# List scatters tied to matmul groups, spectral tiles with pairs of rows innermost, and a new step order

## The chip, the cores and the metric

The kernel runs on one core of a Trainium2 chip. The metric is the time of one execution on the device in microseconds (us); lower is better. The core has five engines that run side by side and meet only through semaphores: TensorE (PE; its weight loads are listed apart as PEld), VectorE (DVE), ScalarE (ACT), GpSimd (POOL) and SyncE (SP). SP, ACT and POOL also issue the transfers between the chip's memory and SBUF, the memory on the core. Matmul results go to PSUM, of which the program uses eight banks of 128 partitions by 512 floats.

## The reference

The kernel computes two things in a row, all in 32-bit floats. First a spectral layer over `x` (8 sequences of 1856 rows of 256 floats):

```python
X = np.fft.rfft(x, axis=1)
Yr = Xr @ w_r - Xi @ w_i + b_r
Yi = Xr @ w_i + Xi @ w_r + b_i
# both soft-thresholded: sign(Y) * max(|Y| - 0.01, 0)
y = np.fft.irfft(Y, n=x.shape[1], axis=1)
```

Then a mixture of experts over the 14848 rows of `y`: each row picks the best of 4 groups and in it the best of 4 experts by two small products and softmaxes; its expert computes `relu(row @ w1) @ w2` (256 to 1024 to 256), and the result is scaled with the two softmax weights.

## The kernel before

**Spectral part.** The sequences are taken in four pairs (`pr`). A sequence of 1856 is 58 by 32, so the transforms become two steps of small matmuls with a transpose between them. Forward: `lead_mm` (letter c in the order, `a_mm` there) multiplies with the 58-point table into two PSUM banks; `turn_a` (d) transposes each bank on VectorE in blocks of 32 into the tile `zys[pr]`, whose free axes are frequency row k (32), sequence of the pair (2) and channel (128). Then for each of 15 pairs of rows k: `f_mm` (e) with the table T; `f_high`, `f_neg`, `f_low`, `f_lneg` (f, g, h, i) split the result into a rounded high part and a rest; `m_bias` (j) and `m_mm` (k), 24 matmuls with the weights' high and low parts; two thresholds `m_relu` (m, n) on ScalarE and their difference `m_sub` (o) on VectorE, written back into `zys`. Backward: `b_mm` (r), its transposes `b_turn` (s) into the tile `vs`, whose axes are row r, sequence, channel; and `p_mm` (v). `p_out` (w) stores the rows to memory (`ys_d`), `p_turn` (x) transposes them, `p_copy` (y on ScalarE, z on VectorE) copies them out.

**Routing.** `g_mm` (G) computes the choice's scores for half a pair, `g_turn` (H) transposes them, and `route_g` (R, one small operation per letter) picks group and expert and counts, for each row, its place in its expert's list. `scatter` (S) then writes one column of 128 rows (row number and weight) into the lists in memory (`lst`) with an indirect DMA on POOL; there are 16 for half a pair and 128 in all. At most three are on their way: each waits for the third one before it to land.

**Early jobs and the rest.** Before all pairs are routed, eight jobs of 256 rows for experts 0 to 3 start from the first entries of the lists: `list_load` (I, on SP), `list_convert` (Z), `e_fetch` (F, two indirect DMAs on POOL), `e_turn` (T), `e_high`, `e_low` (X, Y), `up_mm` (U), `up_high`, `up_low` (A, B), `down_mm` (D), `down_act`, `down_add` (E, J) and `down_out` (K, an indirect DMA on POOL). `w_high` and `w_low` (W, V) split the experts' weights; `load_steps` (l) loads inputs and weights on SP. `last_lists` (L) loads the final lists, `first_rows` (M) fetches the first rows of the job that follows. After the order's end a list of jobs over all 16 experts runs, written in program order (lines 1088 to 1140).

**What sets the order.** The string `ORDER` is a list of 1694 letters; each runs the next step of its kind. A step's instructions are put on TensorE, ScalarE, VectorE and SP in just this order. POOL is not among the engines ordered by hand (`engines`, line 542): its instructions follow the program too, but a scatter starts when its inputs are there and the third scatter before it has landed. So a letter S says when a scatter is written down, not how far TensorE is when it starts. At the start, before the order, the first pair's transposes and the tables are made: T is zeroed and filled by POOL from `traw` in three slices of rows (line 357), `wl`, the low part of the weights, is computed on POOL at line 371.

Of the kernel before, what the change touches and what calls it, by code (L numbers as in the profile page):

```python
# [42 lines left out]
jhdicmnReldfokghjdiRRcnRmRedfovghjkwdwRiRSRvSmnSxweowSzxjxzSxfzkyShgiSSvmSnewokwSjSfSghcmSixnldSeydjcSofxgShkydidcmneldf
ocghjkdiddcnmeldfovghjkwdwivnmewoxwxzjxzkfghivmnewokwjfghGmniojxzfezgxHxyhkyRiRRRRRRvRmRnRewRokwRRjRRfRRgRhvmRRieRwRRwRr
nxfskogyhjsiRxmRxzneRyxojkyRRfRgRhrmRSRiensSfsroSgjGsSshSrHiSesRrsSRRkSRsRSsRRSRRrmRSnRkRSsRfRogSjRhSRriRsmSRneRsfSkRRgo
jRhRisrRmnesfoRkghjsiRemRnvRRfokwRghwRijRSRxmxzSenzfvSoghjkSwwSiSxmxSzenzSfvogShjkwwSiSSxmxzenSzfvoSghjkwSwSixmxzenzfvoI
ghjGwwixHxyZkRyRRRRRRRRvmRnRkRwowRfRRRgxRhmvyRiRxwRRkwzRnRRoRvmnRRwwoxxRFyxRyxRyRyrRFRGssWSWVrWHSWVTSWRsWTRsSWrVWSsXRsSr
RYSsRsrSRRsSRsrSRVSRlUsSRsrARSVRURsSRsSrARRBWSsUWRBWRsUWRRAVvRXBARVwRwxxyBRyRVvRlYDwRwVRvVRxVwDwzRVvWRWlRSVUWVSWVUEVSAJl
# [73 lines left out]
def spectral_moe(ctx: ExitStack, tc: tile.TileContext, x, wri, bri, wgate, w1, w2, cst, out):  # L122
    nc = tc.nc
# [114 lines left out]
    pend, sent = [], []  # L238
# [79 lines left out]
    def new_z():  # L318
        return big.tile([128, KP, 2, 128], F32, name="big")
# [16 lines left out]
    def turn_a(pr, i, bt, o):  # L336
        return nc.vector.transpose(out=zys[pr][:, :, bt, i * 16:i * 16 + 16].rearrange("p k d -> p d k"),
                                   in_=o.rearrange("p (r d) -> p d r", d=16))
# [858 lines left out]
```

## Time and profile before

| what | value |
|---|---|
| median of 3 runs | 1264.16 us (1260.18 to 1267.79) |
| profiled execution, its own time | 1264.4 us |
| its span, first to last instruction | 1262.6 us |
| TensorE busy | 1180.3 us, 93% |
| VectorE busy | 706.8 us, 56% |
| ScalarE busy | 599.5 us, 47% |
| POOL busy | 398.1 us, 32% |
| TensorE clock granted, mean | 0.963 |

The page gives each engine's busy time, then the same in 40 slices of 31.6 us, among them the clock that TensorE was granted. Matmuls overlap, so TensorE's busy share says little on how much work it does; the number of instructions in a stretch says more. A timeline row gives an instruction's start, its length, its engine and line, and in brackets the engine's idle time before it with what ended it: another engine's instruction, a DMA, "remote" (something that is no instruction of the program) or "issue" (nothing that the profile shows). L462 and higher up to L531 are the listed experts, L808 to L831 the early jobs, L244 the scatters.

### The profile page before, as it was taken

The numbers are of one execution on the slowest core, as the hardware profiler recorded it, in microseconds if no ns is written. First come the engines' busy times: TensorE is split into PE (matmuls) and PEld (weight loads), VectorE is DVE, ScalarE is ACT, GpSimd is POOL, SyncE is SP. The second block draws the span as 40 slices with busy tenths as digits, with TensorE's granted clock in tenths as the row PEclk, the third lists the DMA queues.
The fourth block names the chain that finished last, engine by engine and source line by source line (L and its number), as shares of the span: only waits on it lengthen the run. The fifth ranks groups of instructions, "written<-read, shape, count | busy, mean of one in ns | idle before, by whom it ended". The sixth has DMA issues, their size and how long they took to land. (4 is left out here: it accounts for less than half of the span.)

```text
span 1262.6 us, 20533 instructions
## 1 busy us (share of the span) xinstructions
PE 1180.3 (93%) x7620; PEld 963.0 (76%) x7620; DVE 706.8 (56%) x1525; ACT 599.5 (47%) x1435; POOL 398.1 (32%) x447
## 2 busy tenths in 40 slices
PE   8999999989989496689999999999999999999996
PEld 4897786758677173478888888887887988888886
DVE  5657767735855485343557465455455473474452
ACT  2675574547556144132346455444454463463442
POOL 3000005230441515664442434333333323433421
PEclk8999999979989698899999999999999999999998
DMA  9300420122012053303133243452452445335300
GB/s 382 113 1 1 151 118 2 68 84 101 18 52 86 16 204 103 96 18 104 55 117 133 82 165 110 161 190 88 160 194 94 146 143 202 121 126 219 118 26 27
DMA packets 42361, 138.70 MB, mean 110 GB/s; under 512 B 17446, under 2 KB 19756, under 8 KB 31890
## 3 DMA queue, kind: packets, MB, share of 16 engines
q1 hardware_dynamic: 21458, 88.95, 19.7%
q0 software_dynamic: 15904, 31.48, 7.5%
q10 hardware_dynamic: 4896, 16.92, 3.4%
q8 instruction: 61, 1.00, 0.3%
q14 instruction: 42, 0.34, 0.1%
HBM read 103.24 MB, written 35.00 MB: 109 GB/s over the span
## 5 line engine op out<-in xcount | busy, mean ns | idle before, releaser
L523 PE MATMUL py<-big,hh 128*128 128x512 f32 x824 | 298.7, 403 | 0.0
L462 PE MATMUL ph<-xth,big 128*128 128x384 f32 (+1 forms) x896 | 256.9, 362 | 2.6 <-DVE hl L468 1.6
L244 POOL DMA_INDIRECT lst<-ent,sloti x128 | 128.2, 1001 | 353.7 <-DVE mx_g L160 176.1
L524 PE MATMUL py<-big,hl 128*128 128x256 f32 x824 | 231.6, 281 | 0.0
L468 DVE SCALAR_TENSOR_TENSOR hl<-ph,hh 128x256 fp32r<-128x256 f32 x448 | 151.3, 380 | 79.6 <-ACT hh L466 69.0
L523 PEld LDWEIGHTS py<-big,hh 128*128 128x128 f32 x824 | 155.0, 188 | 37.7 <-issue 3.2
L462 PEld LDWEIGHTS ph<-xth,big 128*128 128x128 f32 x896 | 165.1, 188 | 23.4 <-PE ph L462 2.7
L466 ACT ACTIVATE hh<-ph 128x256 fp32r<-128x256 f32 x448 | 137.9, 373 | 84.9 <-PE ph L462 80.8
L462 PE MATMUL ph<-xtl,big 128*128 128x384 f32 (+1 forms) x448 | 161.5, 361 | 0.3 <-DVE xtl L450 0.3
L509 POOL DMA_INDIRECT out_dram<-yo,si_f x96 | 97.6, 1017 | 184.4 <-DVE yo L531 158.9
L524 PEld LDWEIGHTS py<-big,hl 128*128 128x128 f32 x824 | 154.9, 188 | 0.1
L429 POOL DMA_INDIRECT xg<-ys_d,gi_f x96 | 93.6, 975 | 181.6 <-PE pg L445 158.0
L530 ACT ACTIVATE yo<-py,ent_f 128x256 f32<-128x256 f32 x96 | 45.6, 475 | 194.0 <-PE py L524 153.8
L531 DVE SCALAR_TENSOR_TENSOR yo<-py,ent_f,yo 128x256 f32<-128x256 f32 x96 | 46.4, 483 | 162.6 <-ACT yo L530 113.8
L642 PE MATMUL pw<-wh,xh 128*128 128x256 f32 x480 | 126.5, 300 | 2.3 <-issue 2.1
L642 PE MATMUL pw<-wl,xh 128*128 128x256 f32 x480 | 120.3, 287 | 1.8 <-issue 1.7
L642 PEld LDWEIGHTS pw<-wh,xh 128*128 128x128 f32 x480 | 93.8, 195 | 22.9 <-issue 12.7
L412 DVE TENSOR_TENSOR big<-xt,big 128x512 fp32r<-128x512 f32 x160 | 109.1, 682 | 0.0
L411 ACT CAST big<-xt 128x512 fp32r<-128x512 f32 x160 | 104.3, 652 | 0.0
L642 PEld LDWEIGHTS pw<-wl,xh 128*128 128x128 f32 x480 | 93.9, 196 | 2.3 <-issue 2.3
L462 PEld LDWEIGHTS ph<-xtl,big 128*128 128x128 f32 x448 | 84.2, 188 | 8.2 <-DVE xtl L450 0.6
L671 DVE STREAM_TRANSPOSE big<-bank 128x512 f32<-128x512 f32 x64 | 65.8, 1067 | 33.7 <-remote 21.7
(196 smaller groups left out, 1872.2 us busy)
## 6 DMA issues: line engine op xcount, KB each, us to landing
xt<-in_w_dram SPq DMA_DIRECT2D x48, 1024.0 KB
ys_d<-ysb ACTq DMA_DIRECT2D x32, 512.0 KB
big<-in_w_dram SPq DMA_DIRECT2D x16, 1024.0 KB
big<-in_x_dram SPq DMA_DIRECT2D x8, 1024.0 KB
xt<-in_x_dram SPq DMA_DIRECT2D x8, 1024.0 KB
lst<-ent,sloti POOLq DMA_INDIRECT x128
lst<-zero SPq DMA_DIRECT2D x1, 1920.0 KB
xg<-ys_d,gi_f POOLq DMA_INDIRECT x96
```

The lines of the kernel that those rows point to most:

```text
L244: ins = nc.gpsimd.indirect_dma_start(out=lst, out_offset=bass.IndirectOffsetOnAxis(ap=sl_, axis=0), in_=en_, in_offset=None, bounds_check= ...
L411: nc.scalar.copy(out=wt[:, 2 * i, cs], in_=raws[i][:, cs])
L412: nc.vector.tensor_tensor(out=wt[:, 2 * i + 1, cs], in0=raws[i][:, cs], in1=wt[:, 2 * i, cs].bitcast(F32), op=ALU.subtract)
L429: ins = nc.gpsimd.indirect_dma_start(out=xg[:, c, :], out_offset=None, in_=ys_d[0:rows, :], in_offset=bass.IndirectOffsetOnAxis(ap=ids.gi[ ...
L462: nc.tensor.matmul(o[:, :n], lhsT=a_[:, ch, fs], rhs=b_[:, ch, 0:n], start=k == 0, stop=k == 5)
L466: nc.scalar.activation(out=hh[:, f, :m], in_=ov, func=AF.Relu)
L468: nc.vector.scalar_tensor_tensor(out=hl[:, f, :m], in0=ov, scalar=0.0, in1=hh[:, f, :m].bitcast(F32), op0=ALU.max, op1=ALU.subtract)
L509: ins = nc.gpsimd.indirect_dma_start(out=out, out_offset=bass.IndirectOffsetOnAxis(ap=ids.si[:, t:t + 1], axis=0), in_=ysb, in_offset=None ...
L523: nc.tensor.matmul(o, lhsT=hh[:, f, ts], rhs=w2b[:, :, f, :], start=f == 0, stop=f == 7, skip_group_check=True)
L524: nc.tensor.matmul(o[:, 0:D], lhsT=hl[:, f, ts], rhs=w2h[:, f, :], start=False, stop=f == 7, skip_group_check=True)
L642: nc.tensor.matmul(y[:, kp * D:(kp + 1) * D], lhsT=a_[:, c0:c0 + 128], rhs=w_[:, ri, ch, :], start=False, stop=fin, skip_group_check=True)
L671: nc.vector.transpose(out=vs[pr][:, :, bt, j * 16:(j + 1) * 16].rearrange("p r d -> p d r"), in_=psum["b", pr, j][bt].rearrange("p (k d) - ...
```

## The change

1. A list `pace` holds the name of the last matmul of the latest step among `m_mm`, `b_mm`, `p_mm`, `up_mm` and `down_mm`. Each scatter gets a dependency on it, so that it waits on POOL until that matmul has ended.
2. The tiles `zys` and `vs` get two rows innermost: their axes are now pair of rows, sequence, channel, row of the pair. The transposes `turn_a` and `b_turn` write runs of two floats; `f_mm` takes its weights and `p_mm` its moving rows in steps of two floats; `b_mm` reads runs of 32 floats instead of 16; `m_sub` reads both inputs alternating between their halves and writes one run.
3. POOL fills only T's first slice before it computes `wl`; the two later slices follow it.
4. All of `ORDER` is replaced. It has the same counts of each letter, but for one copy that goes from z to y.

```diff
-jejejlfghflgheikiemknfoghjiemknfoghjiemknfoghjicmnedfocghjkdiddcmnedfocghjkdiddcmnedfocjhgkdiddcmnedfocjhgkdiddemknfojhg
...
-nxfezwkhwoigjxnxzxmzeyojxfvzghGwwixHxyeRzvRRRRkRwRwRRRRRRxRmvRznRfxokwzwhjRiRgRReRmRRnvRfxowkhwygijxmxzxnzeyojGfghrHiRse
-sRkRRRRRrmRSRRnkRsRSjofsSghSrRiRmRSResnSsrfogjkShSsiRsSRrRmSRnResSRjorfSsgkhSRisSsRSRrRmRRSnResforjhgksissRRRcmRnedfRkog
...
-BxKADzwSwBxSxzxSyUzSUASBxASvzBSGwwSxSHxyDRzSRRSRvERRRSJwRDwRKRSRvRRRRxwRDRwRzRRxIREvRRyJRKxwDWzwVxWZxzWFxVDWVWVWRFRVWlVW
-VEyFVyRTlJGXRFRYRTHUFRRRTRAURRBSRURSARRRBSRAURFBDRXRRAYSRBTSURRRSRRURARKRRBDSARSUBESJRUAKBSRDXRAYSDRBSRTRWSURWVSWRVUWSRV
-WVDWSVWVSWDVEVSAADBESBJUSJSUAKBDXSAYDSBSUEKJUASBSDABSUEKJUSABSDXASYDBKSDEJSDKDEJKDLTEUJKUABAUBUMABDAXBYDDEJUKUABDABUEJKU
-ABDABDDEJKDEJK
+ejjejlfghflgheikiemknfoghjiemknfojhgiemknfoghjicmnedfocghjkdiddcmnkdfogdjhcmienddcjofedgdchkdidcmnedfdcjogkddhienkmfoghj
...
+gjximxzxnzkyojfghxnvzmiGowwjxHxyeRRyRvRfRRghewwvRRiRxRwewzxRRvRzRxRwRkRwzRRRRRRRxmxzxnkzyjofghGmniojReHfRkghRiRReRmRknRf
+SRojRhgRirmSnesRjorfRsSgkhsisSRRrRmRRnesfSorjhgkRisSRssrRmSnesRjorfsSgkhsisSRRrRmRRnResfSorjhgksiRsSsRRcRmRSnefdRkogjhSd
...
+gjhReiRnRSRvRmRfkwowhSgijxmxSzRnezfRkogRjhIRiRemRRvnRfRokwhSwZigSjxnxSzkmzfoSghSiGnmSokHSRRRSRRRRmRSRnRoSRrRRRSRsRWrsSWR
+VWRVSWRsWRWRrSsWRRWsSsrRSsRRFsRrVsFsVrRlVTssXrYsURsrRAVRTWsUWRsSWRBvWVASUVwwBlSVxAxVyUSByVvVXSAlYDwBSwUWSWVWVUWVSAVvABlS
+BxwUwzSvASBxUwzSwxASxzxyBDySxESvyJGwSwKxHxyDRRyIRRRvRRRDRwRwRvREZRJFxRwRDwRRzRFxRRxRyxRRyDRyKTFEvXJYRDWFWVWVUWVWKVTWVTlF
+WUVWVwVRDwFRlARxABxEByUyRJRKUARRBSGARXBSYDHSRRURRSRRRURARSRTBADSRBRRUSERRRJURSARRBDRASRRXRBDSYRTWSUWVWVSUWVWVSRDWVWVSWVR
+DEVARSABRUSBRJUKRARKBDARRXSBDYSEUJESJUASBTAUSBUASBDASXBDYSUSDSDSDASBDSUSUASBAUSBKXAYKBULUEJEKDJKDDAEBADJEBKJUKDABUEJMDAB
+DEJDDDKKEJEKJK
@@ scatter
             if len(sent) > 2:
                 tc.add_manual_dep(ins.ins, sent[-3], landed, reason="at most three scatters are on their way")
+            if pace:
+                tc.add_manual_dep(ins.ins, pace[-1], landed, reason="scatters keep their places among the steps")
@@ new_z, turn_a
-        return big.tile([128, KP, 2, 128], F32, name="big")
+        return big.tile([128, KP // 2, 2, 128, 2], F32, name="big")
...
-        return nc.vector.transpose(out=zys[pr][:, :, bt, i * 16:i * 16 + 16].rearrange("p k d -> p d k"),
+        return nc.vector.transpose(out=zys[pr][:, :, bt, i * 16:i * 16 + 16, :].rearrange("p k d q -> p d k q"),
                                    in_=o.rearrange("p (r d) -> p d r", d=16))
@@ tables
-    for k in (slice(0, 6), slice(6, 18), slice(18, 30)):
+    def t_blocks(k):
         for h in range(2):
             nc.gpsimd.tensor_copy(out=T[64 * h:64 * h + 64, k, 64 * h:64 * h + 64], in_=traw[64 * h:64 * h + 64, k, :])
+
+    t_blocks(slice(0, 6))
...
     nc.gpsimd.tensor_tensor(out=wl, in0=wraw, in1=wh.bitcast(F32), op=ALU.subtract)
+    t_blocks(slice(6, 18))
+    t_blocks(slice(18, 30))
@@ f_mm
-                nc.tensor.matmul(ov, lhsT=zys[pr][:, 2 * k + kp, bt, :], rhs=T[:, 2 * k + kp, :], start=True, stop=True,
+                nc.tensor.matmul(ov, lhsT=zys[pr][:, k, bt, :, kp], rhs=T[:, 2 * k + kp, :], start=True, stop=True,
@@ m_mm (likewise in b_mm, p_mm, up_mm and down_mm, with ins = the step's last matmul)
+        pace[:] = [ins.ins.name]
@@ m_sub
-        nc.vector.tensor_tensor(out=zys[pr][:, 2 * k:2 * k + 2].rearrange("p k b d -> p (k b d)"), in0=rp, in1=rn, op=ALU.subtract)
+        rp, rn = [t.rearrange("p (q d) -> p d q", q=2) for t in (rp, rn)]
+        nc.vector.tensor_tensor(out=zys[pr][:, k].rearrange("p b d q -> p (b d) q"), in0=rp, in1=rn, op=ALU.subtract)
@@ b_mm
-        z = zys[pr].rearrange("p k b d -> p k (b d)")
+        z = zys[pr].rearrange("p k b d q -> p k (b d q)")
...
-                nc.tensor.matmul(os[bt][64 * h:64 * h + 64, :], lhsT=TP[rows_], rhs=z[rows_, :, h * 128 + j * 16:h * 128 + j * 16 + 16],
+                ins = nc.tensor.matmul(os[bt][64 * h:64 * h + 64, :], lhsT=TP[rows_], rhs=z[rows_, :, h * 256 + j * 32:h * 256 + j * 32 + 32],
@@ b_turn
-            vs[pr] = big.tile([128, NR, 2, 128], F32, name="big")
-        nc.vector.transpose(out=vs[pr][:, :, bt, j * 16:(j + 1) * 16].rearrange("p r d -> p d r"),
-                            in_=psum["b", pr, j][bt].rearrange("p (k d) -> p d k", d=16))
+            vs[pr] = big.tile([128, NR // 2, 2, 128, 2], F32, name="big")
+        nc.vector.transpose(out=vs[pr][:, :, bt, j * 16:(j + 1) * 16, :].rearrange("p r d q -> p d r q"),
+                            in_=psum["b", pr, j][bt].rearrange("p (k d q) -> p d k q", d=16, q=2))
@@ p_mm
-                                     rhs=vs[pr][rows_, r].rearrange("p b d -> p (b d)"), start=True, stop=True, skip_group_check=True)
+                                     rhs=vs[pr][rows_, r // 2, :, :, n].rearrange("p b d -> p (b d)"), start=True, stop=True, skip_group_check=True)
```

More of the change, by code (lines that the diff above doesn't have):

```diff
@@ L42 @@
-sRkRRRRRrmRSRRnkRsRSjofsSghSrRiRmRSResnSsrfogjkShSsiRsSRrRmSRnResSRjorfSsgkhSRisSsRSRrRmRRSnResforjhgksissRRRcmRnedfRkog
[L43 to L46, printed above, removed]
@@ new lines @@
+SRojRhgRirmSnesRjorfRsSgkhsisSRRrRmRRnesfSorjhgkRisSRssrRmSnesRjorfsSgkhsisSRRrRmRRnResfSorjhgksiRsSsRRcRmRSnefdRkogjhSd
+icmSneldfoRkghjSdiRRcmRSnRedfovghjkwdwRiRSRxmvznSfxoewzwxhvySijxkwzwSgvmSnxweowzxjxzSxfzkyhgiSvmneSwoGwjfSvHghxwkwRzSiRR
+RRRRRxmRSxRxyzenRyovjRSRfkRRRwhwRSiRgRRxRmRxRzenRSycjfoRkldghSdiRcmRSnRkdfRgojhRicdmRnkldjoRdSRcmndSjocdldSdvewwrSfxsgey
+sxhfSryhiegsieSsrGsSsrHRksSRsRRRRRSRrmRRnksfRoSgjRsRRhrmRSiRensfsrogjksShRisSRRrRnRRmReRfkSjoghsiSsRemnRvRfoSkwhwRiRgjRR
+xmxRRSeyznvfogkhwSwijSxmxzenzfvogShjkwiwSxmxzenzSfvoghjkwiSwxmxSzenzfvoghjGSwwixHxSyeRRyRvRRRRkSwRRwRRRRSRxRmRxRzknRzfSo
@@ L236, in route_g @@
         yield
-    pend, sent = [], []
+    pend, sent, pace = [], [], []
     landed = mybir.DependencyInfo(mybir.DependencyClass.Sync, mybir.DependencyReason.DATA)
@@ L641, in m_mm @@
                             fin = a_ is xl and kp == 1 and ch == 1 and ri == 1
-                            nc.tensor.matmul(y[:, kp * D:(kp + 1) * D], lhsT=a_[:, c0:c0 + 128], rhs=w_[:, ri, ch, :],
+                            ins = nc.tensor.matmul(y[:, kp * D:(kp + 1) * D], lhsT=a_[:, c0:c0 + 128], rhs=w_[:, ri, ch, :],
                                              start=False, stop=fin, skip_group_check=True)
+        pace[:] = [ins.ins.name]
     def m_relu(nm, store, sign):
@@ L663, in b_mm @@
                 rows_ = slice(64 * bt, 64 * bt + 64)
-                nc.tensor.matmul(os[bt][64 * h:64 * h + 64, :], lhsT=TP[rows_], rhs=z[rows_, :, h * 128 + j * 16:h * 128 + j * 16 + 16],
+                ins = nc.tensor.matmul(os[bt][64 * h:64 * h + 64, :], lhsT=TP[rows_], rhs=z[rows_, :, h * 256 + j * 32:h * 256 + j * 32 + 32],
                                  start=True, stop=True)
+        pace[:] = [ins.ins.name]
     @steps_of(pairs, u8, two)
@@ L681, in p_mm @@
                     r = 4 * v + 2 * u + n
-                    nc.tensor.matmul(os[h][64 * n:64 * n + 64, u * 256:(u + 1) * 256], lhsT=AP[rows_, r, :],
-                                     rhs=vs[pr][rows_, r].rearrange("p b d -> p (b d)"), start=True, stop=True, skip_group_check=True)
+                    ins = nc.tensor.matmul(os[h][64 * n:64 * n + 64, u * 256:(u + 1) * 256], lhsT=AP[rows_, r, :],
+                                     rhs=vs[pr][rows_, r // 2, :, :, n].rearrange("p b d -> p (b d)"), start=True, stop=True, skip_group_check=True)
+        pace[:] = [ins.ins.name]
     ysbs, yts, group = {}, {}, []
@@ L807, in up_mm @@
                 for a_, b_ in ((w[0], xth), (w[0], xtl), (w[1], xth)):
-                    nc.tensor.matmul(o[:, i * 256:(i + 1) * 256], lhsT=a_[:, ch, fs], rhs=b_[:, ch, :], start=k == 0, stop=k == 5)
+                    ins = nc.tensor.matmul(o[:, i * 256:(i + 1) * 256], lhsT=a_[:, ch, fs], rhs=b_[:, ch, :], start=k == 0, stop=k == 5)
                     k += 1
+        pace[:] = [ins.ins.name]
     @steps_of(range(len(jobs)), range(0, 8, 2))
@@ L830, in down_mm @@
                              skip_group_check=True)
-            nc.tensor.matmul(o[:, 0:D], lhsT=hid[n][1][:, f, ts], rhs=w2h[:, f, :], start=False, stop=f == 7,
-                             skip_group_check=True)
+            ins = nc.tensor.matmul(o[:, 0:D], lhsT=hid[n][1][:, f, ts], rhs=w2h[:, f, :], start=False, stop=f == 7,
+                                   skip_group_check=True)
+        pace[:] = [ins.ins.name]
     @steps_of(range(len(jobs)), range(2))
```

6 lines of the change are left out of this document (2 added, 4 removed).

## The prediction

> **What bounds the kernel now.** I read the page first, then the busy time in stretches, then the timeline where a stretch is bad, then the groups by shape. The profiled execution took 1264.4 us, of which 1262.6 us are the span, so 1.8 us lie around it; the median of the three runs is 1264.16 us, the same to 0.02%. The sum below starts from 1264.4.
>
> ```profile
> span 1262.6 us, 20533 instructions
> ...
> PEclk8999999979989698899999999999999999999998
> ```
>
> TensorE's granted clock (tenths, 40 slices of 31.6 us) dips between the 7th and the 18th slice, and hardly anywhere behind. So I cut the span where runs of list scatters on POOL begin and end. Columns: stretch, length, busy time and instruction count of PE, PEld, DVE, ACT, POOL, granted clock, DMA share, GB/s.
>
> ```profile
> 22.00:199.00 177.00, 175.59 (x1450) 142.99 (x1450) 116.77 (x190) 110.27 (x241) 1.05 (x1) 0.98 0.26 90
> 199.00:221.00 22.00, 19.86 (x137) 12.96 (x129) 17.05 (x34) 9.36 (x23) 16.12 (x16) 0.92 0.02 1
> 244.00:271.00 27.00, 21.67 (x127) 16.18 (x129) 4.68 (x10) 8.96 (x20) 15.79 (x16) 0.71 0.17 60
> 326.00:350.00 24.00, 23.40 (x165) 14.50 (x166) 19.71 (x45) 9.90 (x23) 16.49 (x16) 1.00 0.02 2
> 360.00:384.00 24.00, 20.29 (x156) 16.49 (x155) 6.91 (x14) 11.96 (x26) 15.38 (x16) 0.86 0.18 64
> 413.00:443.00 30.00, 13.29 (x47) 2.88 (x40) 11.76 (x22) 1.62 (x4) 15.80 (x17) 0.66 0.04 7
> 464.00:493.00 29.00, 27.20 (x236) 21.04 (x229) 17.90 (x43) 14.62 (x30) 17.10 (x17) 1.00 0.50 179
> 493.00:517.00 24.00, 10.57 (x57) 6.53 (x57) 10.91 (x27) 4.89 (x11) 13.80 (x14) 0.72 0.46 156
> 517.00:536.00 19.00, 10.08 (x72) 8.99 (x72) 7.63 (x23) 3.07 (x7) 13.01 (x13) 0.89 0.13 22
> 536.00:579.00 43.00, 35.44 (x213) 31.63 (x213) 19.39 (x36) 14.58 (x28) 25.99 (x27) 0.89 0.06 17
> 579.00:606.00 27.00, 26.89 (x187) 24.77 (x187) 8.55 (x14) 7.64 (x14) 9.01 (x10) 1.00 0.40 122
> 606.00:1262.00 656.00, 642.59 (x3578) 555.23 (x3576) 342.80 (x839) 307.48 (x819) 225.25 (x271) 1.00 0.36 129
> ```
>
> From 606 us on the listed experts run with TensorE busy 98% at clock 1.00. The diff touches nothing there, so these 656 us stay. What can move lies before. In 22 to 199, where no scatter runs, TensorE gets through 1450 instructions in 177 us, 8.2 per us; in 579 to 606, the expert steps of the early jobs, 187 in 27 us, 6.9 per us. Against these two rates the stretches with scatters fall short. A stretch at 8.2 should take 137/8.2 = 16.7 us and takes 22.0, lost 5.3 (199 to 221); 127/8.2 = 15.5 of 27, lost 11.5 (244 to 271); 20.1 of 24, lost 3.9 (326); 19.0 of 24, lost 5.0 (360); 28.8 of 29, lost 0.2 (464). In 413 to 443 the order holds mostly b_mm and their transposes, and 12 transposes at 1.07 us (row below) are 12.8 us of VectorE; lost 30 - 12.8 = 17.2. At 6.9 per us, 517 to 536 loses 19 - 10.4 = 8.6 and 536 to 579 loses 43 - 30.9 = 12.1. Together 63.8 us, 43.1 of them before 464 us. The stretch 493 to 517 loses 24 - 8.3 = 15.7, for another reason (below).
>
> What happens in the bad ones (start, length, engine, line, in brackets the idle time before and its releaser):
>
> ```profile
> 266.61 0.69 ACT L649 ACTIVATE rp<-pw,nlam 128x512 f32<-128x512 f32 x1 [12.31 <-remote]
> ...
> 418.65 0.97 POOL L244 DMA_INDIRECT lst<-ent,sloti  x1 [0.30 <-issue]
> 419.92 0.97 POOL L244 DMA_INDIRECT lst<-ent,sloti  x1 [0.31 <-issue]
> ...
> 431.89 1.04 DVE L671 STREAM_TRANSPOSE big<-bank 128x512 f32<-128x512 f32 x1 [13.30 <-remote]
> ...
> 532.75 0.97 POOL L244 DMA_INDIRECT lst<-ent,sloti  x1 [0.31 <-issue]
> 533.75 0.60 ACT L815 ACTIVATE hh<-ph 128x512 fp32r<-128x512 f32 x1 [11.63 <-remote]
> ```
>
> At 418.65 and 419.92 two scatters of a run that goes on in steps of 1.28 us past 431; VectorE stands for 13.30 us meanwhile, released by something outside the instructions ("remote"). Up to 266.61 ScalarE stands 12.31 us the same way, and up to 533.75 it stands 11.63 and starts 0.03 us after the last scatter of that run has ended (532.75 + 0.97). So the engines stand while scatters go back to back, and go on when the run ends. Why, the profile doesn't say. Not every run does it: the one at 464 lost nothing. The clock of 0.66 to 0.92 in these stretches is the second part of the price.
>
> **The scatter's wait.** Now POOL starts a scatter as soon as its list is routed and the third one before it has landed; its place in the order holds it back nowhere, and sixteen become ready at once (one per list row of a half pair). With the change the scatter also waits for the last matmul of the step m_mm, b_mm, p_mm, up_mm or down_mm that precedes it. Reading the new order, the 128 scatters stand behind 94 different such steps: 65 alone, 25 twos, 3 threes, 1 four. In the spectral part there are mostly two per unit of five to six us, so POOL is taken 2 x 1.28 of 5.5 us and has pauses. The wait also closes a loop: if an engine stands, TensorE soon stands, the next scatter isn't released, the run ends, and the engine goes on after one or two scatters. I take 80% of the 43.1 back: 34 us. Among the early jobs the new order has about one scatter per up_mm or down_mm, whose 12 or 8 matmuls take 1.4 us; POOL has hardly a pause (1.28 of 1.4), only the loop helps: half of 8.6 + 12.1, 10 us. Together -44. Bounds: nothing if density isn't the cause, -64 if all of it comes back. What the wait adds on POOL itself is nothing that counts: POOL works 13 to 17 of the 19 to 30 us even in the stretches with full runs.
>
> What is queued behind a waiting scatter are fetches (xg) of the early jobs and stores of their results. Ahead of the first two fetches the new order puts eleven scatters into some 10 us of TensorE steps (`SRsRWrsSWRVWRVSWRsWRWRrSsWRRWsSsrRSsRRFsRrVsFsVrRlVT`): 11 x 1.28 and four fetch instructions at about 1.28 are 19 us of POOL, and the first e_turn (T) follows two b_mm later. I charge 6 us for it (0 to 10).
>
> **Pairs of rows innermost.** The three kinds of VectorE transposes, groups by shape (count, busy time, mean ns of one, idle before):
>
> ```profile
> L671 DVE STREAM_TRANSPOSE big<-bank 128x512 f32<-128x512 f32 x64 | 65.8, 1067 | 33.7 <-remote 21.7 <-PE bank L664 10.3 <-PE pg L787 1.3
> L337 DVE STREAM_TRANSPOSE big<-bank 128x512 f32<-128x512 f32 x64 | 62.9, 1074 | 12.5 <-PE bank L333 12.5
> ...
> L727 DVE STREAM_TRANSPOSE L<-bank 128x512 f32<-128x512 f32 x8 | 5.7, 706 | 7.0 <-PE bank L719 4.5 <-PE bank L700 2.5
> ```
>
> zys and vs keep two rows next to each other, so the 128 transposes (L337, L671) write runs of two floats, 8 bytes, instead of single floats 1 KB apart. The only transpose that writes a contiguous tile is L727: 706 ns against 1067 and 1074. The difference, 0.36 us over 512 elements, is 0.70 ns each. I take 0.71 for the paired form; the other bound is 1.07, since L337 still reads its bank in steps of 16 floats and b_turn's pairs there lie 32 floats apart. [...]
>
> Where the transposes set the pace is seen in one unit of the order on VectorE's own timeline (x2 is two in a row, from the first start to the last end):
>
> ```profile
> 106.47 1.94 DVE L671 STREAM_TRANSPOSE big<-bank 128x512 f32<-128x512 f32 x2 [1.06 <-PE bank L664]
> 108.28 0.66 DVE L617 TENSOR_TENSOR xl<-pg,xh 128x512 fp32r<-128x512 f32 x1
> 108.86 0.40 DVE L618 TENSOR_TENSOR xl<-pg,xh 128x256 fp32r<-128x256 f32 x1
> 109.19 2.05 DVE L671 STREAM_TRANSPOSE big<-bank 128x512 f32<-128x512 f32 x2
> 111.06 0.70 DVE L655 TENSOR_TENSOR big<-rp,rn 128x512 f32<-128x512 f32 x1
> 112.80 1.07 DVE L671 STREAM_TRANSPOSE big<-bank 128x512 f32<-128x512 f32 x1 [1.04 <-PE bank L664]
> ```
>
> The unit has one m_mm, one f_mm, two b_mm and four transposes and takes 112.80 - 106.47 = 6.33 us. VectorE: 4 x 1.07 + 0.70 (m_sub) + 0.66 + 0.40 (f_low) = 6.04 of them. With 0.71 it falls to 4.6, with m_sub at its worse price (next) to 5.0. TensorE then sets the unit: 24 + 8 + 2 x 8 = 48 instructions at 8.2 per us, 5.85 us. So up to 0.48 us a unit; 112 transposes after pair 0's first 16 are 28 units, 13 us. Some stand in stretches already counted, and 8.2 is itself an average over such units; I take 6 (0 to 13). The first 16 transposes, pair 0's, stand alone at the start:
>
> ```profile
> 8.84 14.14 DVE L337 STREAM_TRANSPOSE big<-bank 128x512 f32<-128x512 f32 x16
> ```
>
> 14.14 us for 16, back to back; 16 x 0.36 = 5.8 less at most, and I take half, -3 (0 to -5.8), as x may still be arriving.
>
> m_sub now reads its two inputs alternating between halves 1 KB apart. No row shows that; as bounds 0.70 us (L655 as it is) and 0.70 + 0.36, the penalty that the scattered write pays. I take the worse, 1.06: 60 x 0.36 = 22 us of VectorE, hidden behind TensorE in the unit above (5.0 of 5.85) and costing nothing on the path. f_mm loads its weights and p_mm reads its moving rows in steps of two floats. No row shows that either. The bounds are no change and the scattered transposes' factor, 1067/706 = 1.51, on 8 instructions of f_mm (1.0 us at 8.2 per us) and 16 of p_mm (2.0 us): 0.51 x (60 x 1.0 + 32 x 2.0) = 63 us. I take no change, as I take it for the pairs of the transposes: the same runs of two.
>
> **The rest.** Four T copies go behind the subtraction that makes wl on POOL; they are the later rows, not needed before the fourth f_mm, and POOL has 1.05 us of work between 22 and 199: 0. One yt copy of 64 goes from VectorE to ScalarE: 0. The order moves the wait for the second list:
>
> ```profile
> 495.94 0.38 SPq L762 DMA_DIRECT2D ent_b<-lst  x1
> ...
> 498.74 0.17 DVE L280 CAST gi_b<-ent_b 128x10 int32<-128x10 f32 x1 [7.51 <-DMA ent_b<-lst]
> ...
> 502.03 0.69 PE L787 MATMUL pg<-K,xg 128*128 128x128 f32 x2 [1.61 <-DMA xg<-ys_d,gi_b]
> ```
>
> The list load issues at 495.94, just behind the run of scatters from 464; its conversion starts at 498.74, and TensorE turns the first fetched rows at 502.03. In that time the old order gives TensorE little to do (I to Z: one p_mm, two p_turn, one down_mm; F to the first T: one p_turn, one down_mm). The new order has three p_turn and one down_mm more between F and T, 20 instructions or 2.5 us, and its scatters for this list stand alone or in twos behind earlier steps, where the run from 464 took all 29 us of its stretch and came out last; I take 6 of the 15.7 us back (0 to 13).
>
> **Sum.** -44 + 6 - 6 - 3 - 6 = -53; 1264.4 - 53 = 1211.4, forecast 1211 us. Its own range goes by the bounds: all of the first term back and nothing for the fetches gives 1264.4 - 64 - 6 - 3 - 13 = 1178; half of it back, a full backlog and no list gain gives 1264.4 - 32 + 10 - 6 - 3 = 1233.
>
> **The rivals.**
> 1. *The two-float steps slow TensorE* (slower). f_mm's weights and p_mm's moving rows come in at the scattered rate, factor 1.51: +63; 1211 + 63 = 1274. It is slower than before once the factor passes 1.43 (0.43 x 124 = 53). For it: VectorE pays this factor for single floats, and no row shows TensorE reading in steps. Against: two floats lie together. [...]
> 2. *Density isn't the cause*: an engine stands whenever it meets any scatter, or the stall moves with the order. For it: the run at 464 had the same density and lost nothing, and 199 to 221 little. Only the other terms are left: 1264.4 + 6 - 6 - 3 - 6 = 1255.
> 3. *The wait takes the stall's place.* Scatters held back late hold the fetches and stores behind them, and TensorE pays 1.28 us for each of the 32 scatters of the last pair: +41, and the full 10 for the first fetches instead of 6: 1211 + 45 = 1256. For it: POOL runs in order and yo has two buffers. Against: POOL has room, 13.8 busy of 24 us even in 493 to 517.
> 4. *The transposes don't get faster* (the change doesn't do what it says there). The 9 us are lost and m_sub's 0.36 lands on VectorE in 28 units, 10 more: 1230.
>
> **Chances.** Forecast 0.53, rival 4 0.10, rival 2 0.14, rival 3 0.11, rival 1 0.08, other mishaps 0.04. About 0.5% (6.3 us) is what a measurement of this kernel tells from no change. Faster by more than that (below 1258): forecast, rival 4, and some two thirds of rivals 2 and 3, 0.80. Slower (above 1270): rival 1 and half of the mishaps and a tail of rival 3, 0.11. Same: 0.09. The range reaches from 1180 down at all of the first term to 1260, which takes in rivals 2, 3 and 4 and leaves out rival 1.
>
> **What would show it.** Right: no idle of over 4 us on ScalarE or VectorE with a "remote" releaser, scatters more than 1.28 us apart up to the early jobs, clock 1.00 in slices 7 to 14; L671 at about 0.71 us; L655 at 1.0; units under 6.0 us apart. Wrong: "remote" idle next to single scatters (rival 2); TensorE before e_turn or POOL's fetch waiting on a scatter for many us (rival 3); the groups L587 and L682 longer than 291 and 399 ns a matmul (rival 1); L671 still 1.07 (rival 4). The prediction is wrong as a whole if the stretch to the first listed expert doesn't end some 50 us before 606.

## The result and the profile after

The changed kernel takes 1203.03 us (median of 4 runs, 1200.87 to 1207.63) where the kernel before, beside it on the same chip, takes 1265.97 (4 runs, 1260.18 to 1273.61): ratio 0.9504, 95% interval 0.9445 to 0.9564, about 63 us less. The forecast was 1211.

One thing has to be said ahead of all else, since no number below can be read without it. The runs of this study fell on three chips, and the kernel before takes another time on each. On chip A (the first four experiments ran there, and the numbers of the result above agree with it) it takes 1264.08 us (7 runs); on chip B 1208.05 (13 runs, 1202.73 to 1212.48); on chip C 1198.58 (7 runs, 1195.69 to 1203.87). Every comparison below is made within one chip, unless it says otherwise. Each chip was used at one or two times only, so "chip" here stands for the chip together with whatever else ran on it then.

From the page of the changed kernel, profiled on the execution of 1202.32 us, its span and the row of TensorE's granted clock:

```profile
span 1200.5 us, 20603 instructions
...
PEclk9999999999999989899999999999999999999998
```

The dips that stood between the 7th and the 18th slice are gone but for two to 0.8. Next, the busy time in stretches, in the columns that the prediction explains (the second and third number are the length and TensorE's busy time with its count).

```profile
22.00:190.00 168.00, 166.56 (x1405) 135.30 (x1404) 99.05 (x184) 109.11 (x238) 1.08 (x1) 1.00 0.27 95
190.00:371.00 181.00, 180.85 (x1567) 140.43 (x1566) 126.15 (x282) 114.93 (x250) 69.11 (x70) 1.00 0.22 71
371.00:393.00 22.00, 14.31 (x71) 4.00 (x69) 17.84 (x42) 6.45 (x13) 15.74 (x15) 1.00 0.31 59
393.00:431.00 38.00, 36.12 (x307) 27.06 (x307) 22.46 (x46) 20.99 (x40) 12.53 (x13) 0.91 0.59 164
424.00:448.00 24.00, 14.18 (x104) 10.38 (x96) 7.88 (x29) 6.18 (x14) 12.95 (x14) 0.79 0.29 94
445.00:540.00 95.00, 85.06 (x585) 75.13 (x583) 45.93 (x97) 34.41 (x68) 57.12 (x57) 0.96 0.27 85
```

From 190 to 371 us TensorE is now busy 180.85 of 181 us although 70 POOL instructions run beside it; the kernel before lost 5.3, 11.5, 3.9 and 5.0 us in its bad stretches there. The worst place left is 424 to 448, and what TensorE waits for there is not a run of scatters but a list. VectorE's row and TensorE's row:

```profile
440.85 0.17 DVE L282 CAST gi_b<-ent_b 128x10 int32<-128x10 f32 x1 [11.05 <-DMA ent_b<-lst]
```
```profile
441.75 0.80 PE L840 MATMUL py<-big,hh 128*128 128x512 f32 x1 [9.82 <-DVE yo L856]
```

VectorE works in the order written out. It stands 11.05 us at the conversion of the second list (the letter Z), whose load waits for the list's last scatter; behind it stands the add (L856) that frees TensorE's bank, so TensorE stands 9.82 us.

The groups by shape that answer to those of the prediction (count, busy, mean ns of one):

```profile
L593 PE MATMUL pg<-T,big 128*128 128x128 f32 x480 | 69.3, 288 | 1.8 <-DVE xl L624 1.4 <-DVE big L339 0.3
...
L680 DVE STREAM_TRANSPOSE big<-bank 128x512 f32<-128x512 f32 x64 | 43.4, 703 | 20.2 <-PE bank L672 18.7 <-remote 0.7 <-PE pg L797 0.6
L339 DVE STREAM_TRANSPOSE big<-bank 128x512 f32<-128x512 f32 x64 | 42.8, 700 | 23.3 <-PE bank L335 23.3
L663 DVE TENSOR_TENSOR big<-rp,rn 128x512 f32<-128x512 f32 x60 | 42.3, 704 | 37.4 <-ACT rn L656 28.7 <-ACT rp L656 4.8 <-issue 3.7
...
L691 PE MATMUL bank<-big,CI 64*64 64x256 f32 x512 | 36.9, 397 | 0.1
```

Both kinds of transposes are at 0.70 us, m_sub (L663) costs 0.704 instead of 0.685, and f_mm (L593) and p_mm (L691) take 288 and 397 ns a matmul where they took 291 and 399. The idle that was put down to "remote" ahead of b_turn's transposes is 0.7 us in all, where it was 21.7, and no idle of over 4 us on ScalarE or VectorE ends with "remote" any more (the longest is 3.15 us, on ScalarE).

### The profile page after: what moved, and what is told of

Its sections match the earlier page's. It is cut to its first block, busy times and chain, and to the rows that moved or that the text cites. A ratio compares the mean times of both kernels' runs of the same rounds, so it can differ in the third digit from the quotient of the medians.

```text
span 1200.5 us, 20603 instructions
## 1 busy us (share of the span) xinstructions
PE 1150.3 (96%) x7620; PEld 950.4 (79%) x7620; DVE 669.0 (56%) x1524; ACT 598.9 (50%) x1436; POOL 398.9 (33%) x447
## 2 busy tenths in 40 slices
DMA packets 42362, 138.70 MB, mean 116 GB/s; under 512 B 17447, under 2 KB 19757, under 8 KB 31891
## 4 chain that ended last, share of the span: by engine, by line
PE 86%; DMA 4%; issue 4%; DVE 2%; POOL 2%; ACT 1%; POOLq 0%; another core or an unknown queue 0%; SPq 0%; ACTq 0%; DVEq 0%
PE ph L468 22%; PE py L529 16%; PE pw L648 15%; PE py L530 8%; PE pg L593 5%; DMA lst<-ent,sloti 3%; PE bank L672 3%; PE bank L335 2%; PE bank L691 2%; PE bank L710 2%; PE pg L451 2%; PE ph L487 2%; POOL lst L244 1%; PE py L1065 1%; PE ph L1048 1%
## 5 line engine op out<-in xcount | busy, mean ns | idle before, releaser
L648 PE MATMUL pw<-wh,xh 128*128 128x256 f32 x480 | 121.8, 293 | 0.0
L648 PE MATMUL pw<-wl,xh 128*128 128x256 f32 x480 | 116.2, 281 | 0.0
L648 PEld LDWEIGHTS pw<-wh,xh 128*128 128x128 f32 x480 | 90.4, 188 | 21.6 <-issue 13.0
L648 PEld LDWEIGHTS pw<-wl,xh 128*128 128x128 f32 x480 | 90.5, 189 | 0.0
L593 PEld LDWEIGHTS pg<-T,big 128*128 128x128 f32 x480 | 61.2, 196 | 22.5 <-issue 20.6
```

Of the source, the lines that this page charges most:

```text
L593: nc.tensor.matmul(ov, lhsT=zys[pr][:, k, bt, :, kp], rhs=T[:, 2 * k + kp, :], start=True, stop=True, skip_group_check=True)
L648: ins = nc.tensor.matmul(y[:, kp * D:(kp + 1) * D], lhsT=a_[:, c0:c0 + 128], rhs=w_[:, ri, ch, :], start=False, stop=fin, skip_group_check ...
```

## The experiments

**One part at a time, on chip A.** Four kernels, beside 7 runs of the kernel before (1264.08 us).

The first takes the wait out of the changed kernel:

```
-            if pace:
-                tc.add_manual_dep(ins.ins, pace[-1], landed, reason="scatters keep their places among the steps")
```

> The changed kernel without the scatter's wait for the preceding matmul group; new order and pairs layout stay. Theory (scatters back to back make the engines stand, the wait spaces them): the runs of scatters 1.28 us apart return, with idle of over 4 us on ScalarE and VectorE, and the time goes back up by most of the 44 us that the prediction gave the wait: 1235 to 1250 us. Rival (density is not the cause, the gain is the new order's): 1200 to 1212 us, no idle of that kind.

Measured: 1266.88 us (1262.79 to 1272.47), ratio to the kernel before 1.0016 (0.9967 to 1.0064). Everything that the change wins is gone: with it 1203.03, without it 1266.88, so on this chip and in this order the wait is worth 63.9 us. That is more than the theory's 32 to 47. The rival that gave the gain to the order alone falls.

The second puts the wait alone into the kernel before (the added lines of the diff that fill and use `pace`, nothing else).

> The kernel before with the scatter's wait alone; old order, old layout. Theory: the stalls go, but the old order was not made for the wait and has up to seven scatters behind one step, so some bursts stay: 1220 to 1240 us. Rival (wait takes the stall's place: TensorE then waits for late lists): 1255 to 1275 us. Rival (density is not the cause): 1264 us with the long idle still there.

Measured: 1236.76 us (1234.70 to 1241.12), ratio 0.9779 (0.9735 to 0.9823): 27.3 us less, as the theory had it. But its trace shows only half of what the theory says. Two stretches of it:

```profile
199.00:222.00 23.00, 20.19 (x140) 12.73 (x139) 19.37 (x40) 10.73 (x26) 15.70 (x16) 0.95 0.02 1
244.00:263.00 19.00, 17.59 (x152) 13.47 (x152) 8.43 (x14) 12.62 (x26) 13.09 (x13) 1.00 0.31 85
```

POOL still works 15.70 of 23 and 13.09 of 19 us here: the scatters are nearly as dense as before, since the old order has many behind one step. The first stretch loses 23 - 140/8.2 = 5.9 us, no less than the 5.3 of the kernel before. The second, as dense, loses 19 - 152/8.2 = 0.5 us, where the kernel before lost 11.5 of 27. So in one place the wait did nothing, and in another the loss went without the scatters being thinned out. That the tie to TensorE counts by itself is an argument from this second stretch alone: the kernel before, too, has a dense run that lost nothing (from 464 us), with no tie.

The third has the pairs layout alone:

```
-        return big.tile([128, KP, 2, 128], F32, name="big")
+        return big.tile([128, KP // 2, 2, 128, 2], F32, name="big")
...
-            vs[pr] = big.tile([128, NR, 2, 128], F32, name="big")
+            vs[pr] = big.tile([128, NR // 2, 2, 128, 2], F32, name="big")
```

with the slices of the diff that go with these tiles; the fourth has only the lines of `ORDER` replaced.

> The kernel before with the pairs layout alone (transposes at 0.70 us); old order, no wait. Theory: units of the spectral part and the first 16 transposes get shorter, 9 us by the prediction: 1250 to 1258 us, the stalls as before. Rival: the layout was worth much more, as VectorE set the pace in more of the spectral part than was counted: under 1240 us. Rival: nothing, as TensorE sets the pace anyway: 1262 to 1266 us.

> The kernel before with the new order alone; old layout, no wait. Theory: the order alone leaves the stalls, and was searched for cheaper transposes, so with 1.07 us transposes it brings little: 1250 to 1268 us, long idle on ScalarE and VectorE as before. Rival (the order is the gain): 1215 to 1235 us.

Measured: pairs alone 1251.03 us, ratio 0.9890 (0.9847 to 0.9932), 13 us less; the order alone 1271.44, ratio 1.0050 (1.0008 to 1.0092), 7 us more and a little above what was expected. Alone, the three parts give -27, -13 and +7, together -33; the change as a whole gives -61 to -63. The other 28 us come from parts that work together. Most likely these are the wait and the order, as that order spreads the scatters over the steps and only the wait makes POOL keep to it; no run has the wait with just one of the other two parts, so this is argued and not shown.

**The scatters left out, and two kernels meant to space them: chip B.** These four ran on another chip than their expectations had in mind.

```
-            ins = nc.gpsimd.indirect_dma_start(out=lst, out_offset=bass.IndirectOffsetOnAxis(ap=sl_, axis=0), in_=en_,
-                                               in_offset=None, bounds_check=ROWS - 1, oob_is_err=False)
...
```

> The kernel before with its 128 list scatters left out; the lists stay zero, so the experts fetch one and the same row and store none of the result, with the same instructions. This is what the scatters cost in all. Theory (most of the 64 us lost in the head are the scatters'; the list wait of 10 to 15 us is theirs too): 1185 to 1205 us. Rival (the engines stand for another reason): over 1240 us with the long idle still there.

> The changed kernel with its scatters left out in the same way (lists zero, no row of the result stored): its floor. Theory (with the wait little is left but the wait for the second list, a gap of TensorE of 9.8 us): 1185 to 1197 us. If the scatters still cost much beside that gap: under 1180 us.

Measured: the kernel before without its scatters 1175.48 us (1174.48 to 1176.23), the changed one without them 1165.92 (1164.52 to 1168.78). The kernel before takes 1208.05 there, so its scatters and the wait for their lists cost 32.6 us on chip B, together with the stores of the result, which fall away with them (123.39 MB are moved instead of 138.70). Without scatters layout and order are worth 9.6 us. Both came out faster than expected; the expectations were made for chip A. The changed kernel itself didn't run on chip B, so what its scatters cost there isn't known.

```
-            if len(sent) > 2:
-                tc.add_manual_dep(ins.ins, sent[-3], landed, reason="at most three scatters are on their way")
+            if len(sent) > 0:
+                tc.add_manual_dep(ins.ins, sent[-1], landed, reason="at most three scatters are on their way")
```

> The kernel before, where each scatter waits for the one ahead of it to land instead of the third one ahead: scatters are spaced, with no tie to TensorE and the old order. If spacing alone cures the stall: no idle of over 4 us on ScalarE and VectorE; the time falls by 25 to 45 us, to 1220 to 1240 us, less what later lists cost. If the tie to TensorE (an engine that stands holds the next scatter back) is what does it: stalls stay, 1255 us or more.

Measured: 1204.79 us (10 runs), ratio 0.9970 (0.9949 to 0.9990). The edit didn't do what it says. From its timeline of POOL, and its page (DMA issues, the last number is the median time to landing):

```profile
205.00 0.97 POOL L244 DMA_INDIRECT lst<-ent,sloti  x1 [0.30 <-issue]
206.28 0.97 POOL L244 DMA_INDIRECT lst<-ent,sloti  x1 [0.30 <-issue]
```
```profile
lst<-ent,sloti POOLq DMA_INDIRECT x128, 4.6
```
```profile
199.00:221.00 22.00, 22.00 (x167) 15.21 (x160) 21.59 (x45) 12.80 (x30) 16.14 (x16) 1.00 0.03 2
```

The scatters still start 1.28 us apart though they take 4.6 us to land, so neither the previous landing nor the third one before it holds them: between 180 and 610 us POOL waits for a landing 5 times, 6.1 us in all, where the next kernel, which keeps the limit of three, does so 36 times, 49.9 us. The likely reason stands in the kernel right below the edit, where each scatter is declared free of the two before it (`declare_no_dep`, for `before in (1, 2)`); this wasn't tested. So what ran is the kernel before with hardly a limit on its scatters, and as such it tells the most of these four. Sixteen scatters run back to back, POOL works 16.14 of 22 us, and TensorE is busy all 22 us at clock 1.00. On chip A the same stretch of the kernel before had TensorE at 19.86 us and clock 0.92. Here the dense run stops nothing.

Later one does, in another way. Rows of POOL (its last scatter and the first store of the result behind it), ScalarE and TensorE:

```profile
511.75 0.97 POOL L244 DMA_INDIRECT lst<-ent,sloti  x1 [0.30 <-issue]
513.03 0.97 POOL L509 DMA_INDIRECT out_dram<-yo,si_b  x1 [0.30 <-issue]
```
```profile
517.53 0.47 ACT L838 ACTIVATE yo<-bank,ent_b 128x256 f32<-128x256 f32 x1 [20.72 <-DMA out_dram<-yo,si_b]
```
```profile
519.27 0.58 PE L808 MATMUL ph<-xth,big 128*128 128x256 f32 x1 [16.14 <-DVE hl L819]
```

In this program POOL's instructions keep the order written. From 492.57 on it issues sixteen scatters in a row; the two stores of early jobs stand behind them and start at 513.03 and 514.31. ScalarE needs a buffer that such a store empties and stands 20.72 us, and with it TensorE for 16.14. So a dense run can cost time on chip B too, through what is queued behind it on POOL; this is the third rival's mechanism, in a kernel without the wait.

The second kernel that was to space the scatters has, with the tile `idle`:

```
...
             sent.append(ins.ins.name)
+            for _ in range(6):
+                nc.gpsimd.memset(idle, 0.0)
```

> The kernel before with six memsets of 256 floats per partition on POOL (some 1.9 us by the one row of that size) behind each scatter: POOL is as busy as before over longer runs, the scatters are 3.2 us apart. If it is the density of the scatters' transfers that makes engines stand: the stalls go, as with one scatter in flight, and the time falls to 1220 to 1250 us. If a busy POOL as such does it: the stalls grow longer, 1270 us or more.

Measured: 1240.88 us (1238.69 to 1242.50), ratio 1.0283 (1.0238 to 1.0329). That lies in the range expected for spaced scatters only by accident, as that range was meant for chip A; here it is 33 us slower. This edit too missed its aim: the memsets run in blocks of 32 and 65 ahead of the scatters that wait for their data, and the scatters stay mostly 1.28 to 1.8 us apart behind them. Its stretches:

```profile
199.00:366.00 167.00, 167.00 (x1444) 131.14 (x1437) 121.94 (x235) 106.42 (x231) 123.79 (x304) 1.00 0.21 68
366.00:404.00 38.00, 0.83 (x7) 0.63 (x6) 2.67 (x13) 2.29 (x5) 21.12 (x22) 0.54 0.02 1
```
```profile
400.76 0.17 DVE L283 CAST gi_a<-ent_a 128x6 int32<-128x6 f32 x1 [41.42 <-DMA ent_a<-lst]
```

With POOL busy 124 of 167 us TensorE is busy all 167, so a busy POOL as such stops nothing either, on this chip. The 33 us are lost later in one piece, 366 to 404, while POOL works off its scatters. VectorE's row says by which wait: it stands 41.42 us at the conversion of the first list, whose load on SP issues at 398.78, behind the last of the scatters that the memsets have delayed (396.12). ScalarE and TensorE stand behind VectorE, TensorE for 37.17 us. The clock reads 0.54 there, on a chip without the stall: here the low clock goes with a TensorE that stands for a list, so in the bad stretches it need not be the cause either.

**The same two kernels on a chip without the stall, and two tries at the list's wait: chip C.** The changed kernel and the one without the wait ran again, to see which explanation holds where the kernel before is fast.

> The changed kernel once more, beside the kernel before. In the runs with the scatters left out the kernel before took 1208 us on the chip of that call, with its scatters still 1.28 us apart, where it takes 1264 us on the chip of the earlier calls. If the stall belongs to a chip: where the kernel before takes some 1264 us, this takes 1203; where it takes some 1208, the wait has nothing to win and only layout and order are left (the 9.6 us between the two kernels without scatters, and what the lists cost): 1185 to 1200 us.

> The changed kernel without the wait once more. Where the kernel before takes some 1264 us: 1265 us as in its first run. Where the kernel before takes some 1208 us: within 10 us of the changed kernel, as dense scatters stall nothing there; if it is 30 us or more above it, the wait wins on that chip too and something else made the kernel before fast.

Measured, beside 1198.58 us of the kernel before: the changed kernel 1183.44 (1182.22 to 1187.74), ratio 0.9883 (0.9844 to 0.9922); without the wait 1179.45 (1179.01 to 1180.52), ratio 0.9842 (0.9809 to 0.9875). Here the change wins 15 us, and the wait wins none of them: the kernel without it is 4 us lower, and the two sets of runs don't overlap. One kernel, the changed one without its wait, on chip A and then on chip C, the same stretches, and the row in which ScalarE starts again (chip A first):

```profile
185.00:210.00 25.00, 17.62 (x109) 11.35 (x108) 9.71 (x25) 6.51 (x15) 15.71 (x16) 0.91 0.02 1
240.00:268.00 28.00, 20.34 (x150) 14.48 (x150) 8.28 (x17) 10.31 (x21) 15.54 (x16) 0.86 0.18 61
```
```profile
187.63 1.13 POOL L244 DMA_INDIRECT lst<-ent,sloti  x1 [164.47 <-DVE base L235]
...
201.28 0.37 PE L591 MATMUL pg<-T,big 128*128 128x128 f32 x1 [1.15 <-issue]
202.69 0.27 PE L591 MATMUL pg<-T,big 128*128 128x128 f32 x1 [1.04 <-issue]
203.43 0.37 PE L591 MATMUL pg<-T,big 128*128 128x128 f32 x1 [0.47 <-issue]
204.82 0.27 PE L591 MATMUL pg<-T,big 128*128 128x128 f32 x1 [1.02 <-issue]
...
210.59 0.69 ACT L654 ACTIVATE rp<-pw,nlam 128x512 f32<-128x512 f32 x1 [16.00 <-remote]
```

And on chip C:

```profile
185.00:210.00 25.00, 25.00 (x198) 18.43 (x198) 19.90 (x49) 14.48 (x33) 16.24 (x16) 1.00 0.02 1
240.00:268.00 28.00, 28.00 (x259) 22.41 (x252) 18.78 (x46) 19.87 (x44) 8.76 (x9) 1.00 0.32 114
```
```profile
187.53 1.13 POOL L244 DMA_INDIRECT lst<-ent,sloti  x1 [164.46 <-DVE base L235]
188.96 0.98 POOL L244 DMA_INDIRECT lst<-ent,sloti  x1 [0.30 <-issue]
...
208.57 0.97 POOL L244 DMA_INDIRECT lst<-ent,sloti  x1 [0.31 <-issue]
...
208.62 0.69 ACT L654 ACTIVATE rp<-pw,nlam 128x512 f32<-128x512 f32 x1 [1.74 <-PE pw L646]
```

Runs of sixteen scatters start at 187.63 (chip A) and 187.53 (chip C) and are over by 208 and 210. On chip C TensorE gets through 198 instructions meanwhile, on chip A through 109, its matmuls coming one at a time a microsecond or so apart with nothing that they wait for ("issue"); ScalarE has stood 16.00 us there and 1.74 here. (In the second stretch, 240 to 268, the two are no longer alike: 16 scatters fall into it on chip A and 9 on chip C.) The whole kernel takes 1266.88 on the one and 1179.45 on the other.

Last, two tries at the 9.82 us of the list's wait, the second with all of the first (of the lines of `ORDER` only the part that changes is shown):

```
-RvREZRJFxRwRDwRRzRFxRRx
+RvRERJxRwRDwRRzRZFFxRRx
```

and in the second one also

```
-xASxzxyBDySxESvyJGwSwKxHxyD
+xASxzSxyBDySxESvyJGwwKxHxyD
...
-            if len(sent) > 2:
-                tc.add_manual_dep(ins.ins, sent[-3], landed, reason="at most three scatters are on their way")
+            if len(sent) > 4:
+                tc.add_manual_dep(ins.ins, sent[-5], landed, reason="at most three scatters are on their way")
```

> The changed kernel with the conversion of the second list (letter Z) and the first fetch behind it moved nine letters later in the order, so that VectorE runs the add that frees TensorE's bank (the gap of 9.82 us up to 441.75) before it waits for the list. The list itself comes no earlier, and TensorE has some 4 us of work before it needs the fetched rows: 0 to 4 us under the changed kernel. If the gap only moves to the transposes of the fetched rows: no difference.

> As the one before, with five scatters in flight instead of three (POOL stood 1.45 and 2.50 us for a landing ahead of the last scatters of the second list) and the last three of these placed up to two steps earlier in the order: the last scatter of that list goes out some 4 us sooner. If the list is what TensorE waits for: 4 to 9 us under the changed kernel. If more scatters in flight bring the stalls back: slower than the changed kernel, with idle of over 4 us on ScalarE and VectorE.

Measured: 1185.41 us (1183.63 to 1186.20) and 1178.82 us (1178.05 to 1181.71), against 1183.44 of the changed kernel: the first makes no difference, the second takes 4.6 us off. TensorE's rows, of the changed kernel on this chip, of the first and of the second try:

```profile
435.99 0.80 PE L840 MATMUL py<-big,hh 128*128 128x512 f32 x1 [11.19 <-DVE yo L856]
```
```profile
438.42 0.69 PE L797 MATMUL pg<-K,xg 128*128 128x128 f32 x2 [6.03 <-DMA xg<-ys_d,gi_b]
```
```profile
416.36 0.90 PE L710 MATMUL bank<-K,ysb 128*128 128x128 f32 x3 [3.59 <-ACT ysb L702]
```

Moving the conversion out of VectorE's way only moves the wait: TensorE then stands 6.03 us for the fetched rows themselves. Only when the last scatters of the list go out sooner does the long gap go (3.59 us is the longest left between 370 and 530), so that here the version with the wait is level with the one without (1179.45). Which of its two parts does it, the places in the order or five scatters on their way, wasn't parted, and on chip A it wasn't run.

## Why the prediction was right, and where it was not

The time is 8 us under the forecast and inside its own narrow range (1178 to 1233). That the wait takes a stall away, and that this is most of the gain, is right where the prediction looked, on chip A. That the total came so close is in part luck: the wait gave some 20 us more than its term, and the other terms, -9 together, gave nothing, as the changed kernel without its wait is level with the kernel before. It was luck, too, that the result fell on a chip where the kernel before stalls: on chip C the same change wins 15 us. The terms, one by one:

- **The scatter's wait, -44.** Undersized. Taking it out of the changed kernel costs 63.9 us, the upper bound (-64); putting it alone into the kernel before wins 27.3. "80% of the 43.1" was too low: from 190 to 371 nothing is lost, and where the b_mm of the bad stretch now stand (371 to 393) VectorE works 17.84 of 22 us, so the stand of 13.30 us that it had among them is gone as well. "Among the early jobs only the loop helps, half of it" was about right: at 6.9 per us the stretch 445 to 540 loses 95 - 585/6.9 = 10.2 us, where the two stretches of early jobs lost 20.7. By the same count the changed kernel loses 95 - 606/6.9 = 7.2 us there on chip C, so most of what is left isn't chip A's stall.

  The step that doesn't hold is "the engines stand while scatters go back to back", taken as what scatters do by themselves. On chips B and C runs as dense stop nothing in the spectral part (TensorE busy 22.00 of 22 us beside sixteen scatters on B, 25.00 of 25 on C). On chip A, how the wait takes the stall away is open. In the changed kernel the spacing of the scatters and their tie to TensorE come together, and the two kernels that were to part them missed their aim. For spacing speaks that the full gain comes only with the order that spreads the scatters; for the tie, the second stretch of the kernel with the wait alone. What else makes the stall belongs to the chip, or to what ran on it then.
- **POOL's backlog ahead of the first fetches, +6.** It cost nothing that shows: the changed kernel's twelve transposes of fetched rows (L797, from 387.6 us on) have no idle of TensorE put down to the fetch ahead of them.
- **Pairs of rows: units, -6; the lead, -3.** Alone 13 us on chip A; with the order and without scatters 9.6 on chip B. The transposes fell to 0.70 us as taken (703 and 700 ns, from 1067 and 1074), which ends rival 4. The lead came nearly as taken, 2.4 us: f_mm starts at 19.84 us, where it started at 22.24 (TensorE's rows, the changed kernel first).

```profile
19.84 2.42 PE L593 MATMUL pg<-T,big 128*128 128x128 f32 x16 [0.32 <-DVE big L339]
```
```profile
22.24 0.46 PE L587 MATMUL pg<-T,big 128*128 128x128 f32 x2 [0.77 <-DVE big L337]
```

  The units didn't come out under 6 us. In the changed kernel VectorE's timeline has the first rows of three units at

```profile
101.55 1.31 DVE L680 STREAM_TRANSPOSE big<-bank 128x512 f32<-128x512 f32 x2 [2.07 <-PE bank L672]
...
107.76 1.31 DVE L680 STREAM_TRANSPOSE big<-bank 128x512 f32<-128x512 f32 x2 [2.04 <-PE bank L672]
...
113.97 0.72 DVE L680 STREAM_TRANSPOSE big<-bank 128x512 f32<-128x512 f32 x1 [2.07 <-PE bank L672]
```

  6.21 us apart, against 6.33 before, with VectorE waiting 2.07 us for TensorE in each. The step that fails: "TensorE then sets the unit, 48 instructions at 8.2 per us, 5.85 us". 8.2 is a mean over steps of many kinds; cut to this one unit, the kernel before has TensorE busy all of its 6.33 us, so as far as its busy time tells TensorE set the pace already. Where the rest of the 13 us comes from wasn't followed up.

```profile
106.47:112.80 6.33, 6.33 (x49) 4.45 (x50) 5.29 (x8) 3.21 (x8) 0.00 (x0) 1.00 0.00 0
```

- **m_sub, +0.36 a call.** It was 0.02 (0.685 to 0.704). The 0.36 was the author's estimate, carried over from the transposes that write single floats 1 KB apart (1067 and 1074 ns against 706 for the contiguous L727); no row of before showed reads in turn. Here m_sub's reading of its two inputs in turn from halves 1 KB apart costs next to nothing, the 0.02 us just named, while the transposes' writes in pairs in place of single floats took 0.36 and 0.37 us off each.
- **The list's wait, -6.** Not won: 9.82 us of TensorE. The reason given was that the scatters for this list stand alone and come out earlier. In the trace the last but three waits 2.50 us for a landing, the next is released by a p_mm (L691), and the last starts at 435.54. The tie to TensorE is the smaller part of this: on chip C the conversion of this list starts at 435.08 us with the tie and at 433.21 without, and without it TensorE still stands 8.56 us at the same place. POOL's rows (chip A):

```profile
430.44 0.97 POOL L244 DMA_INDIRECT lst<-ent,sloti  x1 [2.50 <-DMA lst<-ent,sloti]
431.71 0.97 POOL L244 DMA_INDIRECT lst<-ent,sloti  x1 [0.30 <-PE bank L691]
...
435.54 0.97 POOL L244 DMA_INDIRECT lst<-ent,sloti  x1 [0.31 <-issue]
```

- **The two-float steps of f_mm and p_mm, 0.** Right (288 and 397 ns a matmul, from 291 and 399), which ends rival 1.
- **Rival 2, density isn't the cause.** Wrong for the time on chip A, where its price was 1255, and right in that density alone isn't the cause: dense scatters meet no stall in the spectral part on B and C (the 22.00 of 22 and 25.00 of 25 us above). The signs that were named for telling them apart ("remote" idle beside single scatters) couldn't show this, as all of them come from one chip's trace.
- **Rival 3, the wait takes the stall's place.** Wrong for the time. Its mechanism is real, but not tied to the wait: dense scatters that hold a store behind them cost TensorE 16.14 us on chip B, in a kernel without the wait.
- **Signs.** Of the signs for "right", the idle of over 4 us with "remote" is gone (the longest is 3.15), the clock is 1.00 up to 371 us and the transposes cost what was said (0.70 us); the scatters still come in twos and threes 1.28 us apart with pauses between, and m_sub and the units came out otherwise, as told. The first transposes of the listed experts start at 539.1 us, where they started at 606.2 (the answer for their line, first and last start behind the durations; the changed kernel first):

```profile
L451 PE MATMUL pg<-K,xg x12: 270/272/331, 539.1 to 554.7; 128*128 128x128 f32 x12
```
```profile
L445 PE MATMUL pg<-K,xg x12: 270/272/273, 606.2 to 617.3; 128*128 128x128 f32 x12
```

  That is 67.1 us earlier and not 50; 62.1 of these reach the end, as what follows took 1200.5 - 539.1 = 661.4 us where it took 656.4. That "these 656 us stay" was 5 us off. About half of it is at the start: from 539 to 545 TensorE waits 3.8 us for the first fetched rows and their conversion, where it waited 1.1; the rest wasn't followed up.

## What to carry to other kernels

Before a stall is explained by what runs beside it, look whether the same instructions at the same times stall on another chip: here one kernel ran 1267 us on one and 1179 on another, and a gain of 63 us was worth 15 there. Tying side work to the step that it should follow cost 4 us on the one chip and took 64 us away on the other. The data that such work delivers can come late with or without the tie (TensorE stood 11.19 us with it and 8.56 without, for the same list on chip C), so its last pieces want to go out early. On a queue that works in order, ask also what stands behind a run of small transfers: here two stores behind sixteen scatters held TensorE for 16 us. And when a rate is used as a bound, it has to be that of the very unit: one view of TensorE's busy time over one unit (6.33 of 6.33 us) would have shown who sets its pace.

## What was not expected of the hardware

The chips differ in what they record, too. The page of the changed kernel without its wait has a median time to landing for the scatters on chip C and none on chip A (chip A first):

```profile
lst<-ent,sloti POOLq DMA_INDIRECT x128
```
```profile
lst<-ent,sloti POOLq DMA_INDIRECT x128, 3.3
```

The trace on chip A holds 4,578 records of landings and 7,989 of semaphore updates, that on chip C 8,239 and 11,981, for the same 20,529 instructions. The other traces of chip A, and those of the kernel before and of the changed kernel, are short in the same way (7,957 to 8,614 updates), with the wait and without.

This bears on how the idle times were read. Every one of the traces that are short puts idle time of these engines down to "remote" or "issue" (in the kernel without the wait on chip A 75.7 us of "remote" on ScalarE between 180 and 620 us); on chips B and C no trace has any of either on TensorE, VectorE or ScalarE in that time. So "remote", which the prediction read as something outside the program, may just be a releaser whose record is missing. That the engines stand is not in doubt (109 instructions against 198).

In the two traces of this kernel the records are equal up to the first scatter at 187 us (999 updates and 514 landings each) and short from then on, also among the listed experts (from 607 us on 4,675 updates on chip A; from 523 us on 6,823 on chip C). But there TensorE doesn't stand: on chip A it is busy 643.72 of the 658 us from 607 on. So the loss of records doesn't by itself go with a stall. Whether the missing records and the standing engines have one cause is open: no run here shows it. It isn't known either whether it is the chip itself or what else ran on it at the time.
